# Moving the tiles of an attention and MoE kernel to other places in SBUF, and one lookup of queries

## The chip, the cores and the metric

The kernel runs on one core of one Trainium2 chip. The metric is the device time of one execution in microseconds (us); lower is better. A core has TensorE (PE in the profile, its weight loads PEld), VectorE (DVE), ScalarE (ACT), GpSimd (POOL) and SyncE (SP), which here only issues transfers.

## The reference

Inputs are q, k, v of shape 4 x 8 x 768 x 64 (batch, heads, sequence, head size) and three MoE weights. In numpy, cut to what matters:

```
scores = 0.125 * (q @ k.T)
keep   = (col < n_sink) | ((0 <= row - col) & (row - col < window))   # n_sink 4, window 128
a      = softmax(where(keep, scores, -1e9))
x      = (a @ v), heads side by side                                  # 3072 x 512
out    = ((x @ w_a) * (x @ w_b)) @ w_out                              # 512 -> 1536 -> 512
```

q, k and v are 32-bit floats. The weights are 64-bit floats, which the kernel turns into 32-bit ones itself.

## The kernel before, in words

**Precision.** A product that is to be as good as 32 bits is made of three matmuls of the faster kind fp32r: each operand is split into a high part and the rest (gh and gl, xh and xl, wh and wl), and the products are high x high, high x rest and rest x high. `product` (two blocks of 128 rows, six matmuls) and `products` (four blocks, twelve) issue them.

**Stages.** The 3,072 rows go through in chunks (`CHUNKS`): the first 128 positions of all four batches, then two chunks of two tiles, then four of four tiles, one for each batch. While the MoE of one chunk runs on TensorE, the attention of the next is worked in between in small steps; `PACE` says how many steps belong behind how many slots. `moe` does the first chunk with 512 columns a matmul, `moe2` the next two with 256, and `moe7` the last four. The last of them has no attention beside it. The traced order is kept on TensorE, VectorE, ScalarE and GpSimd (`keep_order`).

**moe7** multiplies by Strassen's scheme in Winograd's form: seven half-size products instead of eight, for each of six pairs of weight blocks and for w_a and w_b. The moving operands are sums of quarters of x, made by `make_ops` and called B11, T1, T2, T3, B21, B22 and T4. TensorE works in slots, and behind each slot it does a piece of projection (`project_piece`, three matmuls of 512 columns, in which gh and gl are the weights and w_o moves):

- B11 with A11, then T1 with S1, into X; then a piece
- T2 with S2, then T3 with S3, into Y; then a piece
- B21 with A12, then B22 with S4, into X; then a piece
- T4 with A22, into Y; then a piece

A11, A12 and A22 lie in SBUF for good. S1 to S4, and w_o0 to w_o8, were sent to DRAM and are fetched again into six tiles (`AWAY`), whose names in the profile begin with r_.

**Places in SBUF.** A pool lays its tags out in the order of their first use, and the pools stand one behind the other: f_op (the tags w_o1 to w_o5, in the order w_o1, w_o4, w_o5, w_o2, w_o3), f_w (two small tiles good and flag, then all other weights), f_c (the masks m1 and mg, then others), the pools of loads and of attention, and f_mo (small tiles bad and mm, then xh, xl, gh, gl). A weight tile has 4,096 bytes in each partition. In moe7 the tags w_o1 to w_o5 hold B11, T1, T2, T3 and B21 (`OP_HOMES`, `new_ops`); B22 and T4 lie in the tile xl (`x12`).

**Queries.** `load_kq` loads keys and queries of a head, the queries into a tile of the tag io, of which there are six (`NIO`); `prep_q` splits them on GpSimd, the high part with `round`, the rest with `rest`. It finds the tile as `self.qr`, which `load_kq` sets. As a rule the load of head h + 2 is issued behind the split of head h + 1. For the third chunk, though, `rest()` in `run` loads head 0 at step 6 (`LOAD_AT`) and head 1 at step 14, and splits head 0 at step 18, in the first of the `moe2` stages. In those stages `convert` makes the sums S1 to S4 of w_a and w_b; for every other pair of blocks that falls to w_b it uses four tiles of the tag io, two for what it loads and two for the high parts.

Of the kernel before, what the change touches and what calls it, by code (L numbers as in the profile page):

```python
# [7 lines left out]
F32 = mybir.dt.float32  # L8
BF16 = mybir.dt.bfloat16
F32R = mybir.dt.float32r  # L10
I32 = mybir.dt.int32
# [8 lines left out]
DM, FF = 512, 1536  # L20
P = 128
# [8 lines left out]
SW = 2 * P + NS  # L30
# [214 lines left out]
class Fast:  # L245
    def __init__(self, tc, ctx, ident, ins, out, chk):
        self.tc, self.nc, self.ident, self.out, self.chk = tc, tc.nc, ident, out, chk
        self.kT, self.kD, self.qT, self.vB, self.vS, self.kq0, self.v0, self.wa, self.wb, self.wo = ins
        pool = lambda name, bufs, **kw: ctx.enter_context(tc.tile_pool(name=name, bufs=bufs, **kw))
        self.op = pool("f_op", 1)  # L250
        self.wp = pool("f_w", 1)
        self.cp = pool("f_c", 1)
        self.ld = pool("f_ld", 1)
        self.sp = pool("f_sp", 2)
        self.at = pool("f_at", 5)
        self.mo = pool("f_mo", 2)
        self.ps = pool("f_ps", 1, space=PSUM)
        self.dr = pool("f_dr", 1, space=DRAM)
        self.away, self.here, self.fetched = {}, {}, 0
        self.x12, self.roomy, self.turns = None, False, dict(s=0, t=0)  # L260
        bad, mm = (self.mo.tile([P, n], F32, tag=t, name=t, bufs=1) for t, n in (("bad", 16), ("mm", 2)))
        good, flag = self.wp.tile([P, 2], F32, name="good"), self.wp.tile([1, 1], I32, name="flag")
        self.small = bad, mm, good, flag
        self.warm()
        self.consts()

    def consts(self):
        nc, cp = self.nc, self.cp
        flat = self.wp.tile([P, 2, P], BF16, tag=HOMES[5 * B], name="flat")
        self.m0, self.identb = flat[:, 0, :], flat[:, 1, :]  # L270
        nc.scalar.copy(self.identb, self.ident)
        self.m1 = cp.tile([P, SW], F32, name="m1")
        self.mg = cp.tile([P, SW], F32, name="mg")
        self.rel = rel = self.at.tile([P, SW], F32, tag="p", name="rel")
        self.col = col = self.at.tile([P, SW], F32, tag="p", name="col")
        it = dict(allow_small_or_imprecise_dtypes=True)
        s, b = slice(P, P + NS), slice(P + NS, SW)
        nc.gpsimd.iota(rel[:, b], pattern=[[-1, P]], base=0, channel_multiplier=1, **it)
        nc.gpsimd.iota(rel[:, :P], pattern=[[-1, P]], base=P, channel_multiplier=1, **it)
        nc.gpsimd.iota(rel[:, s], pattern=[[1, NS]], base=0, channel_multiplier=0, **it)  # L280
        nc.gpsimd.iota(col[:, :P], pattern=[[1, P]], base=0, channel_multiplier=0, **it)
        V = nc.vector
        pin = self.tc.keep_in_program_order
        pin(V.tensor_scalar(col[:, b], rel[:, b], 0.0, BIG, op0=ALU.is_lt, op1=ALU.mult))
        pin(V.tensor_tensor(rel[:, b], rel[:, b], col[:, b], op=ALU.max))
        V.memset(self.m1[:, s], -NEG)
        self.pt = self.sinks = None
        self.wide = False
        self.tri = cp.tile([P, 2, P], BF16, name="tri")
        self.own = cp.tile([P, P], BF16, name="own")  # L290
        self.x0 = [self.mo.tile([P, NK * B * P], F32R, tag=k, name=k, bufs=1) for k in ("xh", "xl")]
        self.wt, self.whole, self.raw, self.wf, self.unchecked = {}, {}, {}, {}, []

    def masks(self, val, first):
# [144 lines left out]
    def load_kq(self, places, h, tag, home="pt"):  # L439
        if h % 2 == 0:  # L440
            self.kr = []
            for b, t0, n, s0, nb, kw, *_ in places:
                shape, name = [P, kw], f"kr{tag}_{h}_{b}"
                kr = self.cp.tile(shape, F32, tag=home, name=name) if kw > DM else self.io(shape, F32, name)
                self.nc.sync.dma_start(kr[:, :kw], self.kT[b, h // 2, :, s0 * KB:s0 * KB + kw])
                self.kr.append(kr)
        qr = self.io([P, NT * P], F32, f"qr{tag}_{h}")
        for b, t0, n, *_, i in places:
            self.nc.sync.dma_start(qr[:, i * P:(i + n) * P], self.qT[b, h, :, t0 * P:(t0 + n) * P])
        self.qr = qr  # L450

    def prep_k(self, places, h, tag):
        ks = self.sp.tile([P, MK], F32R, tag="kh", name=f"ks{tag}_{h}")
# [7 lines left out]
    def prep_q(self, places, h, tag, k, done):  # L461
        nq = sum(n for _, _, n, *_ in places) * P
        x = self.sp.tile([P, NT * P], F32R, tag=("qh", "ql")[k], name=f"{('qh', 'ql')[k]}{tag}_{h}")
        if k == 0:
            self.round(x[:, :nq], self.qr[:, :nq])
        else:
            self.made_last = self.rest(x[:, :nq], self.qr[:, :nq], done[1][:, :nq])
        return [x]

    def prep_v(self, places, m, tag):  # L470
# [1130 lines left out]
```

## Time and profile before

| | us |
|---|---|
| median of 3 runs | 726.43 (725.37 to 726.82) |
| profiled execution | 726.52 |
| its span | 724.8 |
| TensorE busy | 710.8 (98%) |
| VectorE busy | 451.7 (62%) |
| ScalarE busy | 395.8 (55%) |
| GpSimd busy | 346.0 (48%) |

The span goes from the first to the last instruction; the time has the start and end of the execution around it. A timeline row is one run of like instructions on an engine: when it starts, how long it lasts and how many there are. Matmuls are pipelined, so a row's length reaches past the start of the next, and the time that a run of matmuls takes is read from its start to the start of what follows. The granted clock of TensorE was 0.999 of full speed over the span.

### The profile page before, as it was taken

Reading aid. Unit: us, or ns where it says so; the run is one execution under the profiler, and the core shown is the slowest. Engines: PE = TensorE matmul, PEld = TensorE weight load, DVE = VectorE, ACT = ScalarE, POOL = GpSimd, SP = SyncE. Lnnn points to the kernel's source line nnn. Section 1 sums busy time; section 2 is a strip of 40 time slices with the busy share of each in tenths; the row PEclk is TensorE's granted clock in tenths of the full one; section 3 lists DMA queues with packets and bytes.
Section 4 is the critical chain, followed back from the end, with each engine's and each line's share of the span. In section 5 each row is a group of like instructions: output and inputs, shape, how many; then the busy total and the mean of one; then the engine's idle time right before and its main releaser. Section 6 shows DMA issues by size and latency. Waiting matters only on the chain.

```text
span 724.8 us, 14612 instructions
## 1 busy us (share of the span) xinstructions
PE 710.8 (98%) x4952; PEld 632.0 (87%) x4952; DVE 451.7 (62%) x1255; ACT 395.8 (55%) x1173; POOL 346.0 (48%) x366
## 2 busy tenths in 40 slices
PE   9999999999999999999999999999999999999996
PEld 6977778798889978899989999998999998999995
DVE  5899999456876557655547656555765554743322
ACT  5677776366467665555544565554475652444211
POOL 2200000034666794776833877753777723434430
PEclk9999999999999999999999999999999999999999
DMA  8999974179645476777786597776587665599641
GB/s 327 345 348 354 379 251 152 56 241 300 219 163 183 164 254 251 262 261 244 263 274 227 180 312 257 234 257 220 197 297 259 228 229 207 205 315 367 217 147 62
DMA packets 80641, 175.85 MB, mean 243 GB/s; under 512 B 8624, under 2 KB 26032, under 8 KB 80560
## 3 DMA queue, kind: packets, MB, share of 16 engines
q1 hardware_dynamic: 73504, 162.27, 65.3%
q10 hardware_dynamic: 7056, 12.59, 4.6%
q8 instruction: 41, 0.67, 0.4%
q14 instruction: 40, 0.33, 0.1%
HBM read 144.93 MB, written 29.88 MB: 241 GB/s over the span
## 4 chain that ended last, share of the span: by engine, by line
PE 85%; DVE 5%; DMA 4%; POOL 3%; ACT 1%; issue 1%; SPq 0%; ACTq 0%; DVEq 0%; POOLq 0%
PE o L1225 18%; PE b L921 7%; PE a L921 7%; PE o L948 4%; PE av L754 4%; PE s L709 4%; PE o L998 3%; PE s L823 2%; PE t L742 2%; PE X_0b L1178 2%; PE X_3b L1178 2%; PE X_2b L1178 2%; PE X_3a L1178 2%; PE X_2a L1178 2%; PE X_4a L1178 2%; PE X_1b L1178 2%
## 5 line engine op out<-in xcount | busy, mean ns | idle before, releaser
L1225 PE MATMUL o<-r_O,gh 128*128 128x512 f32 x288 | 97.3, 406 | 0.0
L722 ACT ACTIVATE p<-p,st 128x132 f32<-128x132 f32 x128 | 51.6, 403 | 67.5 <-DVE st L720 67.5
L1352 POOL TENSOR_TENSOR gl<-bu,gh 128x512 fp32r<-128x512 f32 x46 | 60.0, 1305 | 54.4 <-ACT gh L1349 53.5
L719 DVE COPY_PREDICATED s<-own,s 128x128 f32<-128x128 uint16 x128 | 36.7, 287 | 51.3 <-PE s L709 50.8
L736 ACT ACTIVATE p<-p,st 128x132 f32<-128x132 f32 x128 | 44.9, 398 | 30.1 <-DVE st L734 30.1
L1225 PE MATMUL o<-r_O,gl 128*128 128x512 f32 x144 | 56.6, 393 | 1.2 <-POOL gl L1352 1.2
L1053 POOL TENSOR_TENSOR s_a<-s_a 128x256 f32<-128x256 f32 x2 | 1.5, 738 | 116.1 <-DVE x L900 112.0
L425 POOL TENSOR_TENSOR ks<-kr,ks 64x656 fp32r<-64x656 f32 x32 | 51.8, 1619 | 2.7
L1274 POOL TENSOR_TENSOR bu<-x 128x256 f32<-128x256 f32 x24 | 18.6, 777 | 67.5 <-DVE x L1273 61.5
L1225 PEld LDWEIGHTS o<-r_O,gh 128*128 128x128 f32 x288 | 46.2, 188 | 2.7 <-issue 2.1
L425 POOL TENSOR_TENSOR ql<-qr,qh 128x512 fp32r<-128x512 f32 x32 | 41.6, 1300 | 1.3
L744 DVE TENSOR_TENSOR pt<-t,tri 128x1024 f32<-128x1024 f32 x32 | 39.0, 1220 | 5.0 <-PE t L742 4.8
L720 DVE CUSTOM_DVE_ANT_0 p<-s,mg 128x132 f32<-128x132 f32 x128 | 37.7, 295 | 4.4
L422 POOL TENSOR_SCALAR ks<-kr 64x656 fp32r<-64x656 f32 x32 | 24.1, 752 | 32.9 <-PE s L709 27.2
L921 PE MATMUL a<-x,w_a 128*128 128x256 f32 x288 | 39.2, 285 | 0.3 <-DVE x L906 0.3
L1349 ACT CAST gh<-bu 128x512 fp32r<-128x512 f32 x48 | 29.4, 612 | 17.0 <-PE o L1225 8.8
L921 PE MATMUL b<-x,w_b 128*128 128x256 f32 x288 | 38.4, 283 | 0.0
L921 PEld LDWEIGHTS a<-x,w_a 128*128 128x128 f32 x288 | 35.8, 189 | 1.3 <-DVE x L906 0.5
L709 PE MATMUL s<-ks,qh 128*128 128x260 f32 x128 | 36.5, 285 | 0.4 <-DVE st L720 0.4
L709 PE MATMUL s<-ks,ql 128*128 128x260 f32 x128 | 36.2, 283 | 0.0
L921 PEld LDWEIGHTS b<-x,w_b 128*128 128x128 f32 x288 | 35.3, 189 | 0.3 <-issue 0.2
L1355 POOL TENSOR_TENSOR bu<-bu,av 128x512 f32<-128x512 f32 x23 | 30.6, 1332 | 8.3 <-DVE bu L1288 7.9
(490 smaller groups left out, 2213.4 us busy)
## 6 DMA issues: line engine op xcount, KB each, us to landing
r_O<-d_O SPq DMA_DIRECT2D x36, 512.0 KB, 4.4
r_H_a<-d_H_a SPq DMA_DIRECT2D x24, 512.0 KB, 5.2
r_L_a<-d_L_a SPq DMA_DIRECT2D x24, 512.0 KB, 6.1
r_H_b<-d_H_b SPq DMA_DIRECT2D x24, 512.0 KB, 5.0
r_L_b<-d_L_b SPq DMA_DIRECT2D x24, 512.0 KB, 5.7
qr<-in_qT_dram SPq DMA_DIRECT2D x32, 256.0 KB, 3.8
raw_a<-in_wa_dram SPq DMA_DIRECT2D x12, 512.0 KB, 7.1
raw_b<-in_wb_dram SPq DMA_DIRECT2D x12, 512.0 KB, 6.7
```

The source lines that it names most:

```text
L425: return self.nc.gpsimd.tensor_tensor(o, i, high.bitcast(F32), op=ALU.subtract)
L709: mm = nc.tensor.matmul(ps, lhsT=q[:, i * P:(i + 1) * P], rhs=ks[:, c0s[i]:c0s[i] + SW], start=n == 0, stop=n == 1)
L719: nc.vector.copy_predicated(ps[:, :P], self.own.bitcast(mybir.dt.uint16), ps[:, W:])
L720: nc.vector.tensor_tensor_reduce(out=p, in0=ps[:, :W], in1=self.mg[:, :W], scale=-0.125, scalar=BIG, op0=ALU.add, op1=ALU.min, accum_out=s ...
L722: nc.scalar.activation(p, p, AF.Exp, bias=st[:, 0:1], scale=-1.0, accum_out=st[:, 1:2])
L736: nc.scalar.mul(p[:, k, :], p[:, k, :], st[:, 3, k:k + 1])
L744: nc.vector.tensor_tensor(self.parted(nt)[:, h % 2].rearrange("p (c m) q -> p c m q", m=2), tp.unsqueeze(2).to_broadcast(shape), self.tri. ...
L921: mm = self.nc.tensor.matmul(ps[:, cols], lhsT=w[:, ksl], rhs=x[:, kk, cols], start=start and kk == 0 and i == 0, stop=kk == NK - 1 and i ...
L1178: mm = self.nc.tensor.matmul(ps, lhsT=a[:, ksl], rhs=b[:, kk, :], start=start and kk == 0 and n == 0, stop=kk == 1 and n == 2, skip_group_ ...
L1225: self.nc.tensor.matmul(outs[t], lhsT=g[:, sl], rhs=w, start=j == 0 and n == 0, stop=j == NJ - 1 and n == 2)
L1352: (V if late else G).tensor_tensor(hl[k][1], halves[k], hl[k][0].bitcast(F32), op=ALU.subtract)
L1355: (V if late else G).tensor_tensor(halves[1], halves[1], self.av[:, 2 * HN:], op=ALU.mult)
```

## The change

A new method `lay_out` names tiles of f_op in the order w_o2, w_o3, m1, mg, good, flag, w_o4, w_o1, w_o5 before anything else is laid out. The masks m1 and mg move there from f_c, good and flag from f_w; bad goes from f_mo to the head of f_w. The tiles made for w_o1 to w_o5 in it are used by nothing; they fix the places of these tags. `self.qr` becomes a dictionary by chunk and head, so that `prep_q` of the third chunk's head 0 reads the tile loaded for head 0 and not the one loaded last, that of head 1.

```
+        self.lay_out()
+    def lay_out(self):
+        small = {}
+        for tag in ("w_o2", "w_o3", "m1", "mg", "good", "flag", "w_o4", "w_o1", "w_o5"):
+            n = {"m1": SW, "mg": SW, "good": 2, "flag": 1}.get(tag, 2 * DM)
+            small[tag] = self.op.tile([P, n], I32 if tag == "flag" else F32, tag=tag, name=f"place_{tag}")
+        self.m1, self.mg = small["m1"], small["mg"]
+        bad, mm = self.wp.tile([P, 16], F32, tag="bad", name="bad"), self.mo.tile([P, 2], F32, tag="mm", name="mm", bufs=1)
+        self.small = bad, mm, small["good"], small["flag"][:1, :]
...
-        self.qr = qr
+        self.qr[tag, h] = qr
...
-            self.round(x[:, :nq], self.qr[:, :nq])
+            self.round(x[:, :nq], self.qr[tag, h][:, :nq])
         else:
-            self.made_last = self.rest(x[:, :nq], self.qr[:, :nq], done[1][:, :nq])
+            self.made_last = self.rest(x[:, :nq], self.qr.pop((tag, h))[:, :nq], done[1][:, :nq])
```

## Rows read from the trace of the kernel before

**Rows 1.** Busy time by engine on the page: us, share of the span, instructions.

```profile
PE 710.8 (98%) x4952; PEld 632.0 (87%) x4952; DVE 451.7 (62%) x1255; ACT 395.8 (55%) x1173; POOL 346.0 (48%) x366
```

**Rows 2.** TensorE's longest wait: waiter, releaser, us in total, times, longest.

```profile
PE warm L329 <- DVE m L286: 1.3, 1, 1.3
```

**Rows 3.** The chain of waits on the page, by engine.

```profile
PE 85%; DVE 5%; DMA 4%; POOL 3%; ACT 1%; issue 1%; SPq 0%; ACTq 0%; DVEq 0%; POOLq 0%
```

**Rows 4.** Timeline, TensorE, last chunk: start us, length, line, operation, tiles, shape, count.

```profile
697.03 0.87 PE L1178 MATMUL X_5a<-opw_o,w_a 128*128 128x256 f32 x6
697.74 0.39 PE L1178 MATMUL X_5a<-opw_o,r_H_a 128*128 128x256 f32 x2
...
698.42 0.62 PE L1225 MATMUL o<-r_O,gh 128*128 128x512 f32 x2
...
699.10 0.40 PE L1178 MATMUL Y_5a<-opw_o,r_H_a 128*128 128x256 f32 x2
...
699.81 0.39 PE L1178 MATMUL Y_5a<-opw_o,r_H_a 128*128 128x256 f32 x2
...
700.49 0.62 PE L1225 MATMUL o<-r_O,gh 128*128 128x512 f32 x2
...
701.18 0.87 PE L1178 MATMUL X_5a<-opw_o,w_a 128*128 128x256 f32 x6
701.88 0.39 PE L1178 MATMUL X_5a<-x,r_H_a 128*128 128x256 f32 x2
...
702.56 0.62 PE L1225 MATMUL o<-r_O,gh 128*128 128x512 f32 x2
...
703.25 0.87 PE L1178 MATMUL Y_5a<-x,w_a 128*128 128x256 f32 x6
703.96 0.62 PE L1225 MATMUL o<-r_O,gh 128*128 128x512 f32 x2
```

**Rows 5.** Timeline, TensorE, second MoE stage: two runs of twelve.

```profile
218.96 1.52 PE L921 MATMUL b<-x,w_b 128*128 128x256 f32 x12
220.32 0.28 PE L709 MATMUL s<-ks,qh 128*128 128x260 f32 x1
...
224.25 1.58 PE L921 MATMUL b<-x,w_b 128*128 128x256 f32 x12
225.66 0.28 PE L709 MATMUL s<-ks,qh 128*128 128x260 f32 x1
```

**Rows 6.** Timeline, TensorE, first MoE stage: products with x, six matmuls apart.

```profile
136.91 0.63 PE L921 MATMUL b<-xh,w_b 128*128 128x512 f32 x2
...
138.31 0.63 PE L921 MATMUL b<-xh,w_b 128*128 128x512 f32 x2
```

**Rows 7.** Timeline, TensorE, first stage: projections with w_o1 (52 us), w_o10 (140 us).

```profile
52.20 0.61 PE L948 MATMUL o<-w_o,gh 128*128 128x512 f32 x2
...
52.88 0.61 PE L948 MATMUL o<-w_o,gh 128*128 128x512 f32 x2
...
139.94 0.63 PE L948 MATMUL o<-w_o,gh 128*128 128x512 f32 x2
...
141.34 0.63 PE L948 MATMUL o<-w_o,gh 128*128 128x512 f32 x2
```

**Rows 8.** Timeline, POOL: the lower part of head 0's queries.

```profile
191.70 1.32 POOL L425 TENSOR_TENSOR ql<-qr,qh 128x512 fp32r<-128x512 f32 x1
```

**Rows 9.** Timeline, SP's queue: two stores of one conversion, a load of the next.

```profile
177.73 0.51 SPq L1065 DMA_DIRECT2D d_L_b<-sf_b  x1
...
178.77 0.49 SPq L1048 DMA_DIRECT2D sf_b<-d_F_b  x1
179.99 0.33 SPq L1065 DMA_DIRECT2D d_L_b<-sf_b  x1
```

**Rows 10.** Transfers on the page: queue, operation, count, KB each, median us to landing.

```profile
qr<-in_qT_dram SPq DMA_DIRECT2D x32, 256.0 KB, 3.8
```

**Rows 11.** Timeline, DVE: first use of the next conversion's loads.

```profile
189.32 1.82 DVE L1053 TENSOR_TENSOR sf_b<-sf_b 128x256 f32<-128x256 f32 x1
```

More of the change, by code (lines that the diff above doesn't have):

```diff
@@ L260, in __init__ @@
         self.x12, self.roomy, self.turns = None, False, dict(s=0, t=0)
-        bad, mm = (self.mo.tile([P, n], F32, tag=t, name=t, bufs=1) for t, n in (("bad", 16), ("mm", 2)))
-        good, flag = self.wp.tile([P, 2], F32, name="good"), self.wp.tile([1, 1], I32, name="flag")
-        self.small = bad, mm, good, flag
+        self.lay_out()
         self.warm()
         self.consts()
+    def lay_out(self):
[6 more added lines that the diff above has]
+        self.small = bad, mm, small["good"], small["flag"][:1, :]
     def consts(self):
@@ L271, in consts @@
         nc.scalar.copy(self.identb, self.ident)
-        self.m1 = cp.tile([P, SW], F32, name="m1")
-        self.mg = cp.tile([P, SW], F32, name="mg")
         self.rel = rel = self.at.tile([P, SW], F32, tag="p", name="rel")
@@ L291, in consts @@
         self.x0 = [self.mo.tile([P, NK * B * P], F32R, tag=k, name=k, bufs=1) for k in ("xh", "xl")]
+        self.qr = {}
         self.wt, self.whole, self.raw, self.wf, self.unchecked = {}, {}, {}, {}, []
```

## The prediction, made before the change was run

> **What bounds the kernel now.** I read the shares of busy time first, then TensorE's waits, then the chain of waits, then the timeline of TensorE in three stages. TensorE is busy 710.8 of 724.8 us, the next engine 451.7 [rows 1]; its longest single wait in the whole execution is 1.3 us [rows 2]; and 85% of the chain that ended last is TensorE itself [rows 3]. So a nanosecond taken from, or put on, a matmul anywhere moves the end by about a nanosecond, and what other engines do matters only where it makes TensorE wait.
>
> The reader is then to see in the timeline that the same matmul doesn't always take the same time, although it waits for nothing. In the last chunk, between two projection pieces, stand two products of six matmuls of 256 columns each. From start to start, B11 takes 697.74 - 697.03 = 0.71 us and T1 behind it 698.42 - 697.74 = 0.68; T2 takes 0.71 and T3 behind it 0.68; B21 0.70, B22 0.68; T4, alone in its slot, 0.71 [rows 4]. That is 113 ns a matmul in the short pattern and 118 in the long one. The second MoE stage has both as well: a run of twelve takes 220.32 - 218.96 = 1.36 us, another 225.66 - 224.25 = 1.41 [rows 5]. With 512 columns the first stage takes 138.31 - 136.91 = 1.40 us for six, 233 ns each [rows 6]; projections with w_o1 take 52.88 - 52.20 = 0.68 for three, 227 each, and those with w_o10 (141.34 - 139.94) / 6 = 233 [rows 7].
>
> **The change part by part.** Its first part issues no instruction and takes none away: it moves tiles. From the sizes in the code (a weight tile 4,096 bytes a partition, m1 and mg 1,056 each with padding, good, flag and bad 128 together) the weights and everything in their pool move up by 2,176 bytes. The operand tiles of T1 and T2 move down by 12,288, those of B11, T3 and B21 up by 14,464, 6,272 and 10,368; the split x (xh, xl, and B22 and T4 in it) and the gate parts gh, gl stay. Modulo 512 bytes, the size of one weight block of 128 columns in a partition, every moving operand of the MoE stood 64 below its weights; T1, T2 and x now stand 192 below, B11, T3 and B21 keep the 64. For the projections the gate parts are the weights and stood 64 from the weights in f_w and 0 from w_o1 to w_o5; the 64 becomes 192, the 0 becomes 128 for w_o1, w_o4 and w_o5 and stays for w_o2 and w_o3.
>
> Does such a distance matter? The projections with w_o1 (0 apart) are in the 227 pattern and those with w_o10 (64 apart) in the 233 one [rows 7], which speaks for it. T2 and T3, same distance, same matmuls, one long and one short [rows 4], show that it isn't alone: what ran just before decides too. No row shows a matmul of this kind at 128 or 192, so each term is bounded from both sides by the two patterns:
>
> - T1, T2, B22 and T4 come 4 chunks x 6 steps x 2 halves = 48 times each. If T2 and T4 fall into the short pattern: 2 x 48 x 0.03 = 2.9 us less. If T1 and B22 fall into the long one: 2.9 more [rows 4].
> - The second stage has 2 chunks x 24 = 48 runs of twelve. Taking half of them long: 24 x 0.05 = 1.2 us, either way [rows 5].
> - 264 matmuls of 512 columns with x in the first stage: 233 to 227 ns is 1.6 us less; no row excludes the same step upwards, 1.6 more [rows 6, 7].
> - 864 projection matmuls (576 in the last four chunks, 288 before). A piece of three took 0.68 and 0.69 in the last chunk [rows 4]; I take 230 ns, midway between the patterns, so 3 ns x 864 = 2.6 us, either way [rows 7].
>
> All four sum to 8.3 us less or 8.3 us more. I take four tenths of the gain, 3.3 us. Why that side: the long patterns of rows 4 to 6 all occur at 64 bytes, and the change takes most of these operands away from it; and T1 and B22, which would carry the loss of the first term, run short behind a product that ran long at the same distance, so what ran before protects them, while T2 and T4 have only to gain. Why not more: B11 and B21, the other two that run long, keep their distance, and the distances 128 and 192 are nearer to 64 than to the 0 that ran shortest.
>
> The second part is a lookup: head 0 of the third chunk reads the queries loaded for it rather than those of head 1. The same POOL instructions run on the same shape, the last of them at 191.70 for 1.32 us [rows 8]; the tile that they now read was asked for at the sixth step of that stage and is used at the eighteenth, so it is there. No added wait, then, but the tile is held: its slot, one of six of the tag io, was free as soon as it had landed, and is now held until 191.70 + 1.32 = 193.02. A conversion holds four slots meanwhile and head 1's queries the last, so the next conversion's loads, of which the first went out at 178.77, have to wait until that one's stores, issued at 177.73 and 179.99, have landed [rows 9]. With the 3.8 us that queries take to land [rows 10], used as an estimate for these too, the stores are down at 181.5 and 183.8 at the latest, and the loads issued then have landed at 187.6. Behind the waiting load on SP's queue stand the second load and that of v; what needs the converted tile first is DVE at 189.32 [rows 11]. So it costs nothing, with the work that DVE does before as cover and 1.7 us to spare; without that cover it costs the delay of the first load, 181.5 - 178.8 = 2.7 us, to at most 3, as DVE works in a fixed order and TensorE waits for what stands behind. I take 0.
>
> Sum: the profiled execution took 726.52 us (span 724.8 and 1.7 around it), the median 726.43, so the two agree within 0.1; 726.5 - 3.3 = 723.2 us.
>
> **The rivals.** *Distance doesn't matter*: the pattern is set only by what ran before (a projection piece ahead of B11, T2, B21 and T4, rows 4), and every product stays as it was: 726.4 us, within 0.7. For it: T2 and T3. Against it: w_o1 and w_o10 after the same kind of matmul. The Trainium skill, page TensorE: Matmul & The Clock Gate, section Step-by-step: what each phase is for, sides with this rival: it gives TensorE two independent read ports into SBUF, one for the moving operand and one for the weights, so that loading the next weights takes nothing from the matmul that runs. By that rule the sum of the first part is 0; by the rows above, matmuls with all their inputs ready differ by 5 ns, which the rule leaves without a cause, so it is not the likeliest.
>
> *The new distances are the long ones*: 128 and 192 behave as 64 does or worse, w_o1, w_o4 and w_o5 lose their 227, the second stage settles at 1.41 and the gate parts at 233. At half of the last three terms, (1.2 + 1.6 + 2.6) / 2 = 2.7 us more: 729.2; with all four in full 734.8. For it: from 0 to 64 the time grew [rows 7]. It decides from the point at which more of the shifted products run long than do now.
>
> *The held slot*: the conversion's load lands later than DVE can bear, and TensorE waits up to 3 us near 190 us: 729.5 with nothing gained. Against it: the 1.7 us to spare in the working above.
>
> **How the numbers follow.** Forecast (718 to 725.0) 0.50; no change 0.22; long distances 0.23; held slot 0.05. About 0.2%, 1.45 us, is what a measurement of this kernel tells from no change. The forecast's case is almost all faster than that, no change almost all within, the last two slower: faster 0.50, same 0.23, slower 0.27. The range runs from the full gain, 718.0, to 729.0, just under the price of the two slower rivals, beyond which I leave about 0.13 and below 718 some 0.05. The likeliest case alone has 718.0 to 725.0.
>
> **What would show it.** In the last chunk, where nothing but the MoE runs, T2's and T4's products would go from 0.71 to 0.68 and B11's and B21's stay; T1, T3 and B22 stay at 0.68. Runs of twelve in the second stage would be 1.36 more often, six of the first stage under 1.40. TensorE's own waits stay as they are. The forecast is wrong if the steps of the last chunk keep their length, or if projection pieces come to 0.70; the second part's 0 is wrong if TensorE stands still near 190 us.

## The result, and the profile after

The changed kernel took 730.49 us (729.63 to 730.95, 6 runs), the kernel before 725.9 us beside it: ratio 1.0058, 95% interval 1.0045 to 1.007. It is slower, by 4.6 us, and outside the forecast range, on the side of the rival that the new distances are the long ones.

The profiled execution took 730.73 us, its span is 729.0. Busy time by engine on its page (us, share of the span, instructions), the answer to [rows 1]:

```profile
PE 714.9 (98%) x4952; PEld 634.5 (87%) x4952; DVE 451.0 (62%) x1255; ACT 395.8 (54%) x1173; POOL 346.5 (48%) x366
```

The number of instructions is the same. TensorE is busy 4.1 us more and its weight loads 2.5; the other engines moved by 0.7 or less. The granted clock was 0.999 in both profiled executions, so the clock is not the cause. TensorE's two longest waits in total (waiter, releaser, us, times, longest), which answer to [rows 2]:

```profile
PE av L575 <- ACT pt L564: 1.3, 1, 1.3
PE warm L335 <- DVE place_m L291: 1.3, 1, 1.3
```

No wait grew to the size of the loss, and the chain by engine is TensorE again [rows 3]:

```profile
PE 87%; DMA 5%; DVE 3%; POOL 2%; ACT 1%; issue 1%; SPq 0%; ACTq 0%; DVEq 0%; POOLq 0%
```

So the matmuls themselves became longer. TensorE's timeline in the last chunk, the same half step as in [rows 4] (start us, length, engine, line, operation, tiles, shape, count):

```profile
700.95 0.85 PE L1184 MATMUL X_5a<-opw_o,w_a 128*128 128x256 f32 x6
701.64 0.40 PE L1184 MATMUL X_5a<-opw_o,r_H_a 128*128 128x256 f32 x2
...
702.35 0.63 PE L1231 MATMUL o<-r_O,gh 128*128 128x512 f32 x2
...
703.05 0.40 PE L1184 MATMUL Y_5a<-opw_o,r_H_a 128*128 128x256 f32 x2
...
703.76 0.40 PE L1184 MATMUL Y_5a<-opw_o,r_H_a 128*128 128x256 f32 x2
...
704.46 0.63 PE L1231 MATMUL o<-r_O,gh 128*128 128x512 f32 x2
...
705.16 0.85 PE L1184 MATMUL X_5a<-opw_o,w_a 128*128 128x256 f32 x6
705.85 0.40 PE L1184 MATMUL X_5a<-x,r_H_a 128*128 128x256 f32 x2
...
706.56 0.63 PE L1231 MATMUL o<-r_O,gh 128*128 128x512 f32 x2
...
707.26 0.87 PE L1184 MATMUL Y_5a<-x,w_a 128*128 128x256 f32 x6
707.97 0.63 PE L1231 MATMUL o<-r_O,gh 128*128 128x512 f32 x2
...
708.67 0.51 PE L1184 MATMUL X_5b<-opw_o,w_b 128*128 128x256 f32 x3
```

From start to start: B11 0.69 (before 0.71), T1 0.71 (0.68), T2 0.71 (0.71), T3 0.70 (0.68), B21 0.69 (0.70), B22 0.71 (0.68), T4 0.71 (0.71), and each piece of three projections 0.70 (0.68 to 0.69). T1 and B22, which were to stay short, are long; T3, whose distance to its weights didn't change, is longer too; B11 and B21 are a little shorter.

In the first stage six products with x, 512 columns, go the other way, 137.81 - 136.44 = 1.37 us (1.40 in [rows 6]):

```profile
136.44 0.62 PE L927 MATMUL b<-xh,w_b 128*128 128x512 f32 x2
...
137.81 0.62 PE L927 MATMUL b<-xh,w_b 128*128 128x512 f32 x2
```

The projections with w_o1 lost their short pattern, 52.86 - 52.16 = 0.70 us for three (0.68 in [rows 7]):

```profile
52.16 0.63 PE L954 MATMUL o<-w_o,gh 128*128 128x512 f32 x2
...
52.86 0.63 PE L954 MATMUL o<-w_o,gh 128*128 128x512 f32 x2
```

In the second stage both runs of twelve now take 1.41 us, where one took 1.36 [rows 5]:

```profile
218.91 1.57 PE L927 MATMUL b<-x,w_b 128*128 128x256 f32 x12
220.32 0.28 PE L715 MATMUL s<-ks,qh 128*128 128x260 f32 x1
...
224.28 1.57 PE L927 MATMUL b<-x,w_b 128*128 128x256 f32 x12
225.69 0.28 PE L715 MATMUL s<-ks,qh 128*128 128x260 f32 x1
```

The 4,952 matmuls stand in the same order in both traces, so they can be paired one with one, each taken from its start to the next start. Summed by kind in us, after less before: T1 +0.85, T2 +0.48, T3 +0.92, B22 +0.81, T4 +0.37, B11 -0.14, B21 -0.26; second stage +0.63; projections +1.74; products with x of 512 columns -0.87 (264 by 233.3 - 230.0 ns); the rest, with the waits beside these products, -0.3. That is 4.2 us, the difference of the two profiled executions (730.73 - 726.52).

### The profile page after: what moved, and what is told of

Read it like the earlier page. It is cut to its first block, busy times and chain, and to the rows that moved or that the text cites. A ratio compares the mean times of both kernels' runs of the same rounds, so it can differ in the third digit from the quotient of the medians.

```text
span 729.0 us, 14616 instructions
## 1 busy us (share of the span) xinstructions
PE 714.9 (98%) x4952; PEld 634.5 (87%) x4952; DVE 451.0 (62%) x1255; ACT 395.8 (54%) x1173; POOL 346.5 (48%) x366
## 4 chain that ended last, share of the span: by engine, by line
PE 87%; DMA 5%; DVE 3%; POOL 2%; ACT 1%; issue 1%; SPq 0%; ACTq 0%; DVEq 0%; POOLq 0%
PE o L1231 19%; PE a L927 8%; PE b L927 8%; PE o L954 4%; PE av L760 4%; PE s L715 4%; PE o L1004 3%; PE t L748 2%; PE s L829 2%; PE X_4b L1184 2%; PE X_3b L1184 2%; PE X_2b L1184 2%; PE X_5a L1184 2%; PE X_1b L1184 2%; PE X_2a L1184 2%; PE X_3a L1184 2%
## 5 line engine op out<-in xcount | busy, mean ns | idle before, releaser
L1059 POOL TENSOR_TENSOR s_a<-s_a 128x256 f32<-128x256 f32 x2 | 1.5, 737 | 115.7 <-PE o L954 111.7
L726 DVE CUSTOM_DVE_ANT_0 p<-s,place_mg 128x132 f32<-128x132 f32 x128 | 37.7, 295 | 4.5
```

The source lines that it names most:

```text
L726: nc.vector.tensor_tensor_reduce(out=p, in0=ps[:, :W], in1=self.mg[:, :W], scale=-0.125, scalar=BIG, op0=ALU.add, op1=ALU.min, accum_out=s ...
```

## The experiments

Distance means here, as in the prediction, by how many bytes the moving operand lies below the weights within a partition, at the lower address; the names and expectations of the runs call the same "behind". Remainder means the distance modulo 256. Mean times of a matmul are from start to next start, over all of its kind in the trace, without the intervals that hold a wait or other work (over 130 ns for 256 columns, over 250 for 512). Kernels from e4_distance_0 on have the places of the kernel before, apart from what is shown, and the new lookup.

**e1_lookup_only: the lookup alone.**

```
-        self.qr = qr
+        self.qr[tag, h] = qr
```

> The kernel before with the lookup alone (head 0 of the third chunk reads its own queries), all tiles where they were. Theory (distances made the loss, the lookup costs nothing): 725.9 us, ratio to the kernel before 1.000 within 0.001, T1 and B22 at 0.68 us a product in the last chunk as before. Rival (the slot held longer delays a conversion and DVE behind it): 728 to 730.5, with TensorE standing still near 190 us.

Measured: 726.82 us, ratio 1.0003 (0.9992 to 1.0013). The lookup costs nothing that this run can tell.

**e2_places_only: the changed kernel with the old lookup.**

```
-        self.qr[tag, h] = qr
+        self.qr = qr
```

> The changed kernel with the old lookup. Theory (distances alone): 730.5 us, ratio 1.006, every product of T1, T2, B22 and T4 at 0.71 in the last chunk. Rival (held slot): 726 to 728.

Measured: 730.40 us, ratio 1.0058 (1.0041 to 1.0075). The places of the tiles are the whole loss.

**e3_sums_back: the changed kernel with T1 and T2 back at 64.**

```
-        for tag in ("w_o2", "w_o3", "m1", "mg", "good", "flag", "w_o4", "w_o1", "w_o5"):
+        for tag in ("m1", "mg", "good", "flag", "w_o2", "w_o3", "w_o4", "w_o1", "w_o5"):
```

> The changed kernel with m1, mg, good and flag ahead of all five operand tiles, so that T1 and T2 are 64 bytes below their weights again like B11, T3 and B21; split x and gate parts keep their new distances. Theory (a product's distance modulo 512, with what ran before it, sets its pattern): T1, T2 and with them T3, which kept its distance and grew all the same, fall back to about 115, 116 and 113 ns a matmul, 2.2 us of the loss: 728.3. Rival (T3 grew because of something other than T2 ahead of it, such as the projection pieces, which stay as they are): T3 stays near 117, 729.2 to 730.5.

Measured: 729.19 us, ratio 1.0048 (1.0024 to 1.0073). The time lies 0.9 us above the theory's 728.3 and at the rival's lower edge, so it doesn't decide; the rows do. T1 fell from 118.1 to 115.8 ns, T2 from 117.8 to 115.9, T3 from 116.8 to 114.0, where the rival had it near 117; B22, T4 and the x of the second stage, left at 192, stayed long. T3 came back with T1 and T2, without a change of its own.

**e4_distance_0: good and flag to the pool above the weights, all distances 0.**

```
-        good, flag = self.wp.tile([P, 2], F32, name="good"), self.wp.tile([1, 1], I32, name="flag")
+        good, flag = self.cp.tile([P, 2], F32, name="good"), self.cp.tile([1, 1], I32, name="flag")
```

> The kernel before with the lookup, and good and flag moved from the pool of the weights to that of the masks: every moving operand, and every gate part, is at distance 0 modulo 512 from what it meets. Theory: projections at the 227 ns that w_o1 to w_o5 showed at distance 0 instead of 230 (864 x 3.5 = 3.0 us less), products with x of 512 columns at 227 instead of 233 (1.7 less), 256 columns at 113 throughout (up to 5 less): 716 to 722. Rival (the distance to the weights is no cause, what matters is where the operands themselves lie): operands lie where they did, 725.9.

Measured: 733.74 us, ratio 1.0102 (1.0086 to 1.0119). Both the theory and the rival missed: the kernel before took 726.6 beside it, and this one 7 us more. Distance 0 is the best for the x of 512 columns, 228.7 ns in place of 233.3, and one of the worst for 256 columns, T3 119.9 in place of 113.5. TensorE's timeline in the last chunk:

```profile
702.63 0.87 PE L1179 MATMUL X_5a<-opw_o,w_a 128*128 128x256 f32 x6
703.34 0.40 PE L1179 MATMUL X_5a<-opw_o,r_H_a 128*128 128x256 f32 x2
...
704.06 0.63 PE L1226 MATMUL o<-r_O,gh 128*128 128x512 f32 x2
...
710.41 0.76 PE L1179 MATMUL X_5b<-opw_o,w_b 128*128 128x256 f32 x5
```

T1 takes 704.06 - 703.34 = 0.72 us, and the half step 710.41 - 702.63 = 7.78, against 708.67 - 700.95 = 7.72 in the changed kernel and 703.96 + 0.68 - 697.03 = 7.61 before [rows 4].

**e5_behind_128, e6_behind_256, e7_behind_320, e8_behind_384: further along the same line.** m1 and mg (64 bytes modulo 256) or own (256 bytes) go below the weights; in e6 good and flag leave too. The lines are cut from the four kernels; the comments say which has which.

```
+        for t in ("w_o1", "w_o4", "w_o5", "w_o2", "w_o3"):
+            self.op.tile([P, 2 * DM], F32, tag=t, name=f"place_{t}")
+        self.m1, self.mg = (self.op.tile([P, SW], F32, tag=t, name=t) for t in ("m1", "mg"))     # e5, e8
+        self.own = self.op.tile([P, P], BF16, tag="own", name="own")                            # e6, e7, e8
```

> Own queries, and m1 and mg laid out behind the five operand tiles: all moving operands, split x included, stand 128 bytes behind the weights modulo 512, gate parts 128 from w_o. So far 64 behind gave 113 to 116 ns for 256 columns and 233 for 512 with x, 192 behind 118 and 230, 0 (or 512 behind) 119 to 120 and 229. Theory of one slope (the more bytes behind, the longer 256 columns and the shorter 512): 115 to 117 ns and 231 to 232, about 728 us. Rival (the pattern repeats every 256 bytes): no forecast here, but the same means as the run at 384 behind.

> Own queries, good and flag with the masks, own laid out behind the operand tiles: all moving operands 256 bytes behind. One slope: 118 to 119 ns for 256 columns, 229 to 230 for 512, 730 to 733 us. Rival (repeats every 256 bytes): the same as at distance 0, 119 to 120 and 229, 733.7 us.

> Own queries, own laid out behind the operand tiles: all moving operands 320 bytes behind, which is 64 behind modulo 256. One slope: 118 to 120 ns for 256 columns, 229 for 512, 731 to 734 us. Rival (repeats every 256 bytes): as before, T3 and B22 at 113, x of 512 columns at 233, 726 us.

> Own queries, m1, mg and own laid out behind the operand tiles: all moving operands 384 bytes behind. One slope: 119 to 120 ns for 256 columns, 229 for 512, 732 to 735 us. Rival (repeats every 256 bytes): the same means as the run at 128 behind, about 728 us by its neighbours.

Measured: 735.82 us, ratio 1.013 (1.0101 to 1.016); 734.57, 1.0113 (1.0084 to 1.0143); 726.73, 0.9996 (0.9985 to 1.0008); 736.38, 1.0138 (1.0104 to 1.0172). 256 behaves as 0, 320 as 64, 384 as 128: no slope, but a pattern that comes again every 256 bytes in these three pairs, in which 64 is low. The time at 128, by the theory of a slope near 728, is among the longest of all.

**e9_behind_32, e10_behind_96, e11_all_moved: between the points, and the place itself.**

```
-        good, flag = self.wp.tile([P, 2], F32, name="good"), self.wp.tile([1, 1], I32, name="flag")
+        good, flag = self.wp.tile([P, 2], F32, name="good"), self.cp.tile([1, 1], I32, name="flag")   # e9
+        self.m1 = self.op.tile([P, SW], F32, tag="m1", name="m1")                       # e10, above w_o3
+        self.op.tile([P, 48], F32, tag="ahead", name="ahead")                           # e11, first of all
```

> The gate's flag alone goes to the block behind the weights, so the operand tiles and the x stand 32 bytes behind the weights (modulo 256; 64 in the kernel before). Theory (the remainder of the distance by 256 sets the interval, and runs over it without steps): half way between remainder 0 (733.7 and 734.6) and 64 (726), 730 +- 1.5. Rival (only blocks of 64 bytes count): one of the neighbours' times, 726 or 734.

> One mask tile alone goes ahead of the weights, so the operand tiles and the x stand 96 bytes behind the weights (modulo 256). Theory (the remainder runs without steps): half way between remainder 64 (726) and 128 (736), 731 +- 1.5. Rival (blocks of 64 bytes): 726 or 736. If 64 is not the lowest point of the curve, this run or the one at 32 comes below 726.

> 192 bytes stand ahead of everything: each tile moves, and no distance between two tiles changes. Theory (only the distance counts): as the kernel before, 726 +- 0.7. Rival (the place of a tile in SBUF itself counts, modulo 256, as for the weights, which in all kernels so far began at the same remainder or another with the distances): 730 or more.

Measured: 732.36 us, ratio 1.0074 (1.0056 to 1.0091); 734.84, 1.0116 (1.0092 to 1.014); 725.89, 0.9992 (0.998 to 1.0005). In e11 every place moved and no distance did, and the time stayed: distances count, not places, as far as one shift of 192 bytes shows. But my half-way values failed on both sides, by 2 and 4 us: the low point at 64 is narrow, 32 bytes either way lose most of it.

Mean ns of a matmul by remainder (the column 192 is the changed kernel, where T3 stays at 64; the others move all operand sums, x and gate parts together, so they don't show alone what a product's own distance does; for 0 and 192 e13, e14 and e15 below help to tell them apart, for 32, 96 and 128 no run does):

| remainder | 0 (e4) | 32 (e9) | 64 (before) | 96 (e10) | 128 (e5) | 192 |
|---|---|---|---|---|---|---|
| T1, 256 columns | 119.8 | 118.1 | 114.7 | 118.4 | 119.8 | 118.1 |
| T3, 256 columns | 119.9 | 117.9 | 113.5 | 118.3 | 119.8 | 116.8 (at 64) |
| second stage, 256 columns | 119.4 | 118.3 | 116.3 | 118.3 | 119.0 | 117.4 |
| x, 512 columns | 228.7 | 233.0 | 233.3 | 233.8 | 232.5 | 230.0 |

**e12_first_x_at_0: the best remainder for each form.** Only the split x of the first stage moves to 0; the gate parts above it come to 0 as well. The later tenant of xl is made 64 bytes longer too and keeps its place (not shown).

```
-        self.x0 = [self.mo.tile([P, NK * B * P], F32R, tag=k, name=k, bufs=1) for k in ("xh", "xl")]
+        xl = self.mo.tile([P, 4 * DM + 16], F32R, tag="xl", name="xl", bufs=1)[:, 16:]
+        self.x0 = [self.mo.tile([P, NK * B * P], F32R, tag="xh", name="xh", bufs=1), xl]
```

> The split x of the first stage alone goes to remainder 0 (the two tiles begin 64 bytes later), its later tenant and the operand sums stay 64 bytes behind the weights, the gate parts come to remainder 0. Theory (each form has its own best remainder): 264 products of 512 columns by 228.7 in place of 233.3 ns, -1.2 us; the gate parts' projections between -0.65 and +0.6 us: 724.7, between 724.1 and 725.4, ratio 0.998. Rival (a form's interval belongs to the whole setting, not to its own two tiles): 726 or more, with the 512-column products at 233 ns.

Measured: 727.67 us, ratio 1.0018 (0.9999 to 1.0037): a miss by 3 us, in an interval that just holds no change. The products with x took 228.6 ns, as expected, and the projections of the last four chunks 229.0 in place of 230.3. But T3 took 117.3 ns in place of 113.5, B22 115.9 in place of 113.4, T2 117.6 in place of 116.1, at their old distance.

**e13_gates_at_0, e14_x_at_0_gates_kept, e15_T2_alone: why products grow whose distance is kept.**

```
+        self.mo.tile([P, 16], F32, tag="ahead", name="ahead", bufs=1)                   # e13, above x0
+        for t in ("gh", "gh", "gl", "gl"):                                              # e14, below e12's x0
+            self.mo.tile([P, 2 * HN], F32R, tag=t, name=f"place_{t}")
+        for tag in ("w_o3", "m1", "mg", "good", "flag", "w_o2", "w_o4", "w_o1", "w_o5"):  # e15, paddings keep the rest
```

> From the kernel before, the gate parts alone go to remainder 0 (64 bytes later); the split x and the operand sums stay 64 behind. Theory (the projections set the entry into a run of products, and the products fall to their short interval only from the entry of the kernel before): the 864 projection products gain 1.4 to 2.2 ns each, -1.2 to -1.9 us, the products of a run stay at 117 to 118 ns throughout, 10.2 ns for each group of seven, x 288 = +2.9 us: 727.2 to 727.9. Rival (the x's place did it in the run with the first x at 0): projections gain, products keep 113 ns in the second half of a run: 724.5.

> The split x of the first stage at remainder 0, the gate parts and the operand sums as in the kernel before. Theory: only the 264 products of 512 columns change, 228.7 by 233.3 ns, -1.2 us: 724.9 +- 0.5, ratio 0.998. Rival (the x's place lengthens the products): -1.2 + 2.9: 727.8.

> From the kernel before, T2 alone goes to 192 behind; T1, T3, the others, the x and the gate parts keep their distances. Theory (T3, the second product of T2's run, loses its short interval though its own distance is kept, since a run falls to it only after six products 64 behind): T2 288 x 1.7 ns = +0.5, T3 288 x 3.3 ns = +0.95 us: 727.6 +- 0.5. Rival (T3 grew in the changed kernel through the gate parts or the x, not through T2): +0.5 alone: 726.6.

Measured: e13 730.02 us, ratio 1.0041 (1.0022 to 1.0061); e14 726.19, 0.9982 (0.9965 to 0.9998); e15 727.81, 1.0011 (0.9991 to 1.003).

e13: the gate parts' place, which no operand of the products shares, makes them long. The time is 2 us above the theory's 727.9. Part of that excess comes with the clock: the mean granted clock of five of its ten executions was 0.995 to 0.997 (0.994 to 0.996 in five of 27 of the kernel before); the executions at 0.998 or more have medians of 728.54 and 726.86, 1.7 us apart, where the theory had 1.0 to 1.7 more. In the trace the seven products together take 2.9 us more, as the theory had it, and a projection 1.0 ns less, where it had 1.4 to 2.2. T2 and T3 in the last chunk of e13:

```profile
700.69 0.62 PE L1227 MATMUL o<-r_O,gh 128*128 128x512 f32 x2
...
701.37 0.40 PE L1180 MATMUL Y_5a<-opw_o,r_H_a 128*128 128x256 f32 x2
...
702.08 0.40 PE L1180 MATMUL Y_5a<-opw_o,r_H_a 128*128 128x256 f32 x2
...
702.78 0.62 PE L1227 MATMUL o<-r_O,gh 128*128 128x512 f32 x2
```

and the same two products of the same kernel in the first chunk of the last four:

```profile
389.48 0.63 PE L1227 MATMUL o<-r_O,gh 128*128 128x512 f32 x2
...
390.18 0.41 PE L1180 MATMUL Y_5b<-opw_o,r_H_b 128*128 128x256 f32 x2
...
390.88 0.39 PE L1180 MATMUL Y_5b<-opw_o,r_H_b 128*128 128x256 f32 x2
...
391.22 0.39 PE L1180 MATMUL Y_5b<-opw_o,r_H_b 128*128 128x256 f32 x2
...
391.56 0.63 PE L1227 MATMUL o<-r_O,gh 128*128 128x512 f32 x2
```

At 702.08 T3 takes 0.70 us behind a piece of projections of 701.37 - 700.69 = 0.68; at 390.88 it takes 0.68 behind one of 390.18 - 389.48 = 0.70. So at one and the same distance there are two patterns, and what ran before picks one. I count a product as short when the median of its last four matmuls is under 115.5 ns: T3 is short in 46 of its 48 places in the kernel before, and in 5 of 48 in e13. The attention beside it is not the reason: in the last chunk, which has none, it is 12 of 12 against none. Matmul by matmul, in ns, T2 and then T3:

```
before, last chunk     117 117 117 123 118 114 | 113 113 114 113 113 114
e13 at 390.2           119 124 118 114 113 113 | 114 113 113 114 113 113
e13 at 701.4           118 117 118 118 117 119 | 117 118 118 118 117 118
e15, last chunk        117 118 117 119 117 118 | 116 116 114 114 113 113
changed, last chunk    117 116 122 117 118 118 | 114 119 117 118 117 121
```

In the kernel before and in e13, where all products are at 64, a run of twelve either comes down to 113 within six matmuls or stays long to its end; which of the two hangs on how it was entered.

e15: T2 alone at 192 loses 1.7 ns itself and lengthens T3 behind it by 2.3 (113.5 to 115.8): +0.48 and +0.70 us in the trace, where 0.5 and 0.95 were expected. The time, by its ratio 0.8 us above the kernel before, lies between the rival's 0.5 and the theory's 1.45, and its interval, which holds no change as well, doesn't tell them apart; the trace does: T3 is short in 24 of 48 places in place of 46, each time behind a T2 that ran at 117 to 119 throughout, and long behind most of those whose T2 went up and down (114 121 119 117 116 122). So the theory's reason, that a run comes down only after six products at 64, is not right as it stands: in the last chunk T3 comes down within its own six. Its rows there: T2 0.71, T3 0.69 where before had 0.68.

```profile
700.87 0.40 PE L1183 MATMUL Y_5a<-opw_o,r_H_a 128*128 128x256 f32 x2
...
701.58 0.40 PE L1183 MATMUL Y_5a<-opw_o,r_H_a 128*128 128x256 f32 x2
...
702.27 0.62 PE L1230 MATMUL o<-r_O,gh 128*128 128x512 f32 x2
```

e14: six products with x take 137.40 - 136.04 = 1.36 us (1.40 before; over all 264 the mean is 228.7 ns), and the products of the last chunk keep their patterns (T1 698.63 - 697.95 = 0.68):

```profile
136.04 0.62 PE L925 MATMUL b<-xh,w_b 128*128 128x512 f32 x2
...
137.40 0.39 PE L925 MATMUL b<-xh,w_b 128*128 128x512 f32 x1
...
697.25 0.87 PE L1182 MATMUL X_5a<-opw_o,w_a 128*128 128x256 f32 x6
697.95 0.39 PE L1182 MATMUL X_5a<-opw_o,r_H_a 128*128 128x256 f32 x2
...
698.63 0.62 PE L1229 MATMUL o<-r_O,gh 128*128 128x512 f32 x2
```

Its median is 0.8 us below that of the kernel before beside it, where 1.2 were expected, and its interval just leaves out no change; its profiled execution, 726.75 us, is not below the 726.52 of the kernel before. That its products with x are shorter is shown, that the whole kernel is shorter only barely.

## Why the prediction was wrong

**The step that failed** is the choice of the sign: "I take four tenths of the gain", because "the long patterns of rows 4 to 6 all occur at 64 bytes, and the change takes most of these operands away from it". All of those operands stood at 64, so the rows held no other distance to compare with; the one comparison, w_o1 at 0 against w_o10 at 64, was of 512 columns, and e4 shows that 512 and 256 columns want different distances. For 256 columns, 64 is the low point of the six remainders tried (e4, e5, e9, e10 and the changed kernel all lie higher). The gate parts moved too in these runs, but they are not all of it: with the gate parts at 0, T1 took 115.7 ns at 64 (e13) and 119.8 at 0 (e4), and T2 alone at 192 lost 1.7 ns (e15). The prediction also counted modulo 512, where e6 to e8 show 256.

**"... what ran before protects them, while T2 and T4 have only to gain"** failed too. T1 and B22 carried 1.66 us of the loss. What ran before does decide between the two patterns (e13), but the operand's own distance has to allow the short one: at 192, T1 stayed at 117 to 119 ns in eleven of the twelve half steps of the last chunk although B11 ahead of it had come down to 113. Of the 4 x 48 = 192 places of T1, T2, B22 and T4 in the changed kernel 2 are short. And the protection works the other way as well: with T2 at 192, T3 at 64 is short in 14 of its 48 places in the changed kernel and in 24 in e15, against 46 before, and came back with T1 and T2 in e3. I had put T3 at no change; it is the largest single product, +0.92 us.

**The terms**, with their bounds: T1, T2, B22 and T4, bounded by 2.9 either way, came to +2.51. That this is near the full loss is chance: the bound was worked out for T1 and B22 alone, which lost 1.66 of it, and the other 0.85 is T2 and T4, for which the prediction had no loss. B11, T3 and B21, put at 0, came to +0.52. The second stage, bounded by 1.2, +0.63. The projections, bounded by 2.6, +1.74. The products with x of 512 columns, bounded by 1.6, -0.87: the one term on the forecast's side. (The full gain is 726.5 - 8.3 = 718.2 by the prediction's own terms, not 718.0; nothing hangs on it.)

**The rival that came** was priced at 729.2 us as half of its last three terms, without the first; the first turned out to be the largest, and one of the three a gain. Its condition, that more of the shifted products run long than do now, was met; the measured 730.49 lies between its 729.2 and its 734.8.

**Distance doesn't matter** fell with e2 (ratio 1.0058) and e5 (735.82 us against 726.52 beside it): e2 changes places alone, and e5 places and the lookup, which costs nothing by e1; e11 shows that it was the distances. By the Trainium skill's two independent read ports (page TensorE: Matmul & The Clock Gate, section Step-by-step: what each phase is for) these runs should have taken the time of the kernel before; the measurements decide against reading the rule that far.

**The lookup at 0** was right (e1), and so was the held slot at 0.05: the lower part of head 0's queries runs at the same place, 191.53 us against 191.70 [rows 8], and no wait near it answers for a loss. The working behind the 0 held as well: the held tile did put off the next conversion's first load, from 178.77 [rows 9] to 180.12, by 1.35 us where 2.7 were worked out, and DVE still began on it at 189.16, where before it was 189.32 [rows 11].

```profile
180.12 0.37 SPq L1054 DMA_DIRECT2D sf_b<-d_F_b  x1
...
189.16 1.82 DVE L1059 TENSOR_TENSOR sf_b<-sf_b 128x256 f32<-128x256 f32 x1
...
191.53 1.32 POOL L431 TENSOR_TENSOR ql<-qr,qh 128x512 fp32r<-128x512 f32 x1
```

What stays open is why a remainder of 64 is short for 256 columns and long for 512, and by what a run takes over its pattern from the one ahead. The runs show that the distance between the moving operand and the weights counts, with a period of 256 bytes, and that what ran ahead counts too; no run tells which part of the chip sees either.

## What to carry to other kernels

In a kernel whose time is TensorE's own, a tile of a few bytes, moved from below the weights to above them, can cost more than most edits gain (a 32-byte tile, 6 us in e9), so fix the places of the operands and compare their distances to the weights modulo 256 in both programs before the arithmetic of anything else. When the same matmul shows two durations, a trace at one distance says nothing of another: bound it from both sides and leave the sign open, or try a few distances, for each width of matmul by itself. Judge a whole run of matmuls, not one, since a run takes over the pattern that it was entered with.

## What the runs showed of the hardware that I had not expected

Matmuls of 256 columns that wait for nothing took between 113.5 and 119.9 ns, as means by kind, by the remainder of a distance and by what ran ahead; those of 512 columns with x 228.7 to 233.8, with another best remainder (0 against 64). Moving everything together changed nothing (e11, 0.9992). And the same product at the same distances ran at 113 or 118 ns a matmul in one execution (e13 at 390.9 and 702.1 us).
